# Joining two attention products and reordering the last gates of a fused attention and feed-forward kernel

## The chip, the core and the metric

The kernel runs on one core of a Trainium2 chip. The core has five engines that run their own instruction queues in order: TensorE (PE in the profile; its weight loads are PEld), VectorE (DVE), ScalarE (ACT), GpSimd (POOL) and SyncE (SP), which here issues most DMAs. TensorE writes its products into PSUM, eight banks of 512 fp32 per partition. The metric is the device time of one execution in microseconds (us), as a median of several.

## The reference

All inputs are fp32 (the kernel gets the feed-forward weights as 64-bit floats and converts them itself). Per batch and head, `k` and `v` (576 x 64) give a 64 x 64 matrix `kv`; `q` times `kv` is divided by its root mean square per row; the heads, side by side, are the rows `x` of the feed-forward block:

```python
kv = np.einsum('bhsd,bhse->bhde', k, v)          # 8 batches, 8 heads, 576 tokens, 64 wide
out = np.einsum('bhsd,bhde->bhse', q, kv)
rms = np.sqrt(np.mean(out * out, axis=-1, keepdims=True) + 1e-06)
x = (out / rms * g_norm)                          # -> (4608, 512)
h = ((x @ w1) * (x @ w2)) @ w3                    # 512 -> 1024 -> 1024
y = h @ w_out                                     # 1024 -> 512
```

## The kernel before, in words

**Groups.** The 4608 tokens are worked off in nine groups of 512 (the last 64 tokens of each of the eight batches make up the ninth). The loop takes them in the order T = 0, 1, 2, 3, 4, 5, 6, 8, 7, so the third to sixth groups are T = 2 to 5. `w3 @ w_out` is folded into one matrix at the start. A group then has two stages: the gates, which multiply `x` with `w1` and `w2` and take the elementwise product of the two into a tile `ab`, and the projection of `ab` with the folded matrix, whose result is stored.

**Strassen.** All large products are done with seven block products in place of eight (Winograd's form), with sums of the operand blocks made by VectorE. Blocks are named a11 to a22 and b11 to b22, sums s1 to s4 and t1 to t4, results c11 to c22. From T = 2 on (`IN_TWO`) part of it is done at two levels:
- first gates (`gates(T, 2)`, one level, matmuls at L708),
- gates of two (`gates_of_two`, two levels, L976): 14 products, n = 0 to 6 for w = 0 and again for w = 1, in five banks of the pool `mm`,
- last gates (`gates(T, 3)`, one level, L708): seven products of eight 256-wide matmul records,
- projection (`project_twice`, two levels, L1223): seven inner products of 28 records.

In a one-level stage (`winograd`) a product goes into a bank, `keep` lets ScalarE copy what is needed later to SBUF (L726), further products are accumulated into the same bank after that, and `done` hands two parts to `multiply`: VectorE adds them (L859) and multiplies the two halves into `ab` (L860). Where only one part is given, ScalarE copies one half (L854) and VectorE multiplies it with the other half in PSUM (L856). The order before is: a11 b11 (kept as p1), s1 t1 (kept as p5), s2 t2 (kept as u2), s4 b22 (gives c12), s3 t3 (gives c22 with p5, read from the bank), a12 b21 (gives c11 with p1), a22 t4 (gives c21).

`sum_ab` and `sum_ab_two` (L1069 to L1072) are the operand sums of the projection's outer level, and `sum_inner` (L1181 to L1185) those of its inner level, four operations for each of the seven products n. In the last gates the list `following` says which of them VectorE does after which result.

**Attention between the products.** While group T is worked on, the attention of batch T + 1 is done in eight steps (`steps`). TensorE's order is written out by hand: `between()` runs the next step, twice in the first gates (steps 0 and 1), four times in the gates of two (2 to 5) and twice in the last gates (6 and 7). `begin_kv(g)` multiplies k and v of four heads (L335) into two banks of the pool `at`, ScalarE copies them to `kv_sb` in six copies (L343, L345), and SP is given the loads of the next k and v (L104). `finish(h)` multiplies q with kv for four heads (L413) into two banks, and `norm` squares them on ScalarE (L380, from batch 3 on with one buffer for both halves), reduces (L381), takes the root (L385) and the reciprocal (L387) and scales (L390). For batches 3 to 7, step 1 does `begin_kv(1)` and `finish(0)`, step 4 `finish(1)`, and step 6 `begin_kv(0)` of the batch after; odd batches do `product_left` (L432) in step 3. Here is the choice of banks:

```python
of_mm = b and not (h and b > FIRST_OF_TWO)
o_ps = [bank(*((ps_mm, "mm") if of_mm else (ps_at, "at"))), bank(ps_at, "at")]
```

From batch 2 on, q and x are turned by a ScalarE copy (L296, L294), a DMA transpose (L298) and a second ScalarE copy (L308). `turns_by_scalar` ties them to copies of the gates through `slots`: in the last gates one x copy (L294) follows p1's copy, one follows p5's, and two q copies (L296) of the next batch follow u2's.

**Who sets the order.** TensorE, POOL and SP run in the order of the program (`manual_schedule`). A planner orders ScalarE, and VectorE as well, except in the last gates and the projection from T = 1 on (for T = 8 and 7 from the gates of two on), where VectorE runs in program order. `mm` has five banks and `at` three, given out in turn; a new tile waits for the last use of the bank's old one.

Of the kernel before, what the change touches and what calls it, by code (L numbers as in the profile page):

```python
# [22 lines left out]
def kernel(  # L23
# [294 lines left out]
    def attention(b):  # L318
# [80 lines left out]
        def product(h):  # L399

            of_mm = b and not (h and b > FIRST_OF_TWO)
            o_ps = [bank(*((ps_mm, "mm") if of_mm else (ps_at, "at"))), bank(ps_at, "at")]
            for m in range(4):
                r, e = 2 * h + m // 2, m % 2
                for i in range(2):
                    n = 2 * m + i
                    for t in range(2):
                        tokens = slice(t * L, (t + 1) * L)  # L410
                        for l in range(2):
                            rows = slice(l * D, (l + 1) * D)
                            nc.tensor.matmul(  # L413
                                o_ps[l][tokens, n * D:(n + 1) * D],
                                lhsT=qT[r][rows, e, i, tokens],
                                rhs=kv_b[rows, m // 2 ^ l, e, h, :],
                                start=True,
                                stop=True,
                            )
            xn = st[h] = work.tile([P, 2, 2, 4, D], FP32, name="xn", bufs=1)  # L420
            return norm(o_ps, [xn[:, :, l].rearrange("p i m d -> p m i d") for l in range(2)])
# [151 lines left out]
    def steps(b):  # L573

        a = batch(b)
        a.start()
        more = b + 1 < B  # L580
        fs, ends = ([[] for _ in range(8)] for _ in range(2))

        def turn(i, f, *args, next_group=False):

            t = []

            def begin():
# [12 lines left out]
        by_scalar, in_two = b >= FIRST_OF_TWO, b > FIRST_OF_TWO  # L600
        if b == 1:
            early.extend(a.q_two_by_dma(r) for r in (0, 1))
            q_first = list(early)
            fs[0].append((a.begin_kv, 0))

            def end_first():
                for t in q_first:
                    with tc.issue_after(copies["u3"][-1].ins):
                        next(t)
                    all_of(t)  # L610

            ends[1].append((end_first,))
        fs[2 if b == 1 else 1] += [(a.begin_kv, 1), (a.finish, 0)]
        if b == 1:
            last = {}

            def begin(name, behind, f, *args):
                last[name] = f(*args)
                with tc.issue_after(copies[behind][-1].ins):
                    next(last[name])  # L620
                next(last[name])

            def end(name, behind):
                with tc.issue_after(copies[behind][-1].ins):
                    next(last[name], None)
                all_of(last[name])

            fs[2] += [(begin, f"q{r}", "u2", a.q_two_by_dma, r) for r in (2, 3)]
            fs[3].append((begin, "left", "u3", a.q_left_by_dma))
            fs[4].append((begin, "x", "u3", a.x_by_dma, 0, nc.scalar.copy))  # L630
            ends[4] += [(end, "q2", "p1"), (end, "q3", "p5")]
            ends[5] += [(end, "x", "u2"), (end, "left", "u3")]
        elif by_scalar:
            turns_by_scalar(b)
        else:
            turn(1, a.q_two_by_dma, 2, 3)
            turn(2, a.x_by_dma, 0)
            if odd:
                turn(1, a.q_left_by_dma)
        second = 5 if b == 1 else 4  # L640
        if more:
            fs[6 if in_two else second].append((batch(b + 1).begin_kv, 0))
        fs[second].append((a.finish, 1))
        if odd:
            fs[3 if in_two else second + 1].append((a.product_left,))
        if b == 1:
            turn(6, a.x_by_dma, 1)
# [49 lines left out]

    def winograd(
        lhsT, rhs, chunks, done, between=lambda: None, keep_u3=True, after=lambda: None,
        places=(2, 1, 0),  # L700
    ):


        def product(a_name, b_name, to=None):
            ps = to if to is not None else bank(ps_mm, "mm").rearrange("p (u n) -> p u n", u=2)
            for u in range(2):
                for c in range(chunks):
                    nc.tensor.matmul(  # L708
                        ps[:, u, :],
                        lhsT=lhsT(a_name, u, c),  # L710
                        rhs=rhs(b_name, c),

                        start=(u == 0 and c == 0 and to is None),
                        stop=(c == chunks - 1),
                        skip_group_check=True,
                    )
            after()
            return ps

        def keep(name, ps):  # L720
            if name == "p1":
                t = pair_of_sums[:, 0].rearrange("p s c t -> p (s c) t")
            else:
                t = late_slots(places[("p5", "u2", "u3").index(name)])
            t = t[:, 0:4, :].rearrange("p (u a) n -> p u (a n)", u=2)
            copies.setdefault(name, []).append(nc.scalar.copy(t, ps))  # L726
            run_slot((stage[0], name), copies[name][-1])
            late[name] = t
            return t

        r1 = product("a11", "b11")
        p1 = keep("p1", r1)
        r2 = product("s1", "t1")
        p5 = keep("p5", r2)
        product("s2", "t2", r1)
        u2 = keep("u2", r1)
        between()
        product("s4", "b22", r2)
# [105 lines left out]
    def gates(T, p, between, ready=lambda name: None):  # L844
# [4 lines left out]
        def multiply(name, one, two):  # L849
# [14 lines left out]
            lambda name, c: xb[T][name][:, c, :],  # L864
            NP // 2, done, between, T == 0 or p + 1 < NF,
            places=(2, 1, 0) if T not in IN_TWO else (0, 1, 2) if p + 1 == NF else (2, 0, 1),
        )


# [287 lines left out]

    inner = {}

    def sum_inner(*ns, between=lambda: None):  # L1160

        x_1 = ab[1].rearrange("p f j n -> p j f n")
        if ns == (1, 2):
            x = two_ab_sums[0]
        elif ns == (5, 6):
            x = x_1
        else:
            n, = ns
            x = {0: ab[0][:, :, 0], 3: ab_sums[2], 4: ab[0][:, :, 1], 6: x_1[:, 1]}[n].unsqueeze(1)
        a11, a12, a21, a22 = (  # L1170
            x[:, :, 2 * j:2 * j + 2, i * P:(i + 1) * P] for i in range(2) for j in range(2)
        )
# [2 lines left out]
        else:  # L1175
            s1, s2, s4 = (
                t.unsqueeze(1) for t in (
                    inner_sums[n % 4 // 3] if n < 6 else [pair_of_sums[:, 0, i] for i in range(3)]
                )
            )  # L1180
        nc.vector.tensor_add(s1, a21, a22)  # L1181
        nc.vector.tensor_sub(s2, s1, a11)
        nc.vector.tensor_sub(s4, a12, s2)
        between()
        nc.vector.tensor_sub(a21, a11, a21)  # L1185
        for i, n in enumerate(ns):
            inner[n] = [t[:, i] for t in (a11, a12, a22, s1, s2, s4, a21)]

    def project_twice(T, last, ahead, load_after):
        def store(half):  # L1190
# [245 lines left out]
    for n, T in enumerate(groups):  # L1436
# [44 lines left out]
        for p in range(NF):  # L1481
# [2 lines left out]
            stage[0] = f"p{p}" if T in IN_TWO or T == FIRST_OF_TWO - 1 else None  # L1484
            if T and p + 1 == NF:
                sum_1, sum_2, sum_4, sum_3 = sum_ab(p)
                following = {
                    "c12": [], "c22": [sum_1], "c11": [lambda: sum_inner(0, between=sum_2)],
                    "c21": [*of_two, lambda: sum_inner(1, 2), sum_3, sum_4],
                }  # L1490
# [100 lines left out]
```

## Time and profile before

| | |
|---|---|
| median of 3 runs | 746.61 us (745.99 to 747.71) |
| profiled execution: its time, its span | 747.45 us, 745.7 us |
| granted TensorE clock | 1.0 |
| kernel instructions in the profile | 16769 |
| ScalarE PSUM to SBUF copy of 128x512 (L726) | 61, 587 ns each |
| ScalarE half copy of 128x256 (L854) | 22, 371 ns each |
| VectorE product of 128x256 from PSUM (L856) | 22, 413 ns each |
| VectorE add of 128x512 (L859, mm and inner_sums) | 22, 688 ns each |
| ScalarE q copy before the transpose (L296) | 26, 1058 ns each |
| group T = 3, from its first matmul to the next group's | 313.54 to 386.52 us |

The page gives the share of each engine, the span in 40 slices, the DMA queues, the chain of work that ended last, and the costliest groups of instructions. The chain follows the last instruction back to what released it; the rows "start, length, what" are that chain in order of time. A timeline row has start, length, engine, line, operation, tiles written and read, and in brackets the idle time of the engine before it with what ended it. fp32 matmuls appear as two records each, and a row that merges several shows their number.

### The profile page before, as it was taken

What the parts mean: (1) busy time and instruction counts of PE and PEld (TensorE: products, weight loads), DVE (VectorE), ACT (ScalarE), POOL (GpSimd) and SP (SyncE); (2) the same over time, 40 slices, a digit from 0 to 9 for tenths busy, and PEclk for the clock granted to TensorE, in tenths of its full rate; (3) what the DMA queues carried; (4) which work ended last, traced back from release to release, by engine and by line L of the source; (5) the groups of instructions that cost most, each with busy time, mean ns of one, the idle gap of its engine ahead of it and who ended that gap; (6) DMA issues with size and microseconds to landing.
All of it is one profiled execution on the core that took longest, in us unless ns stands there. A gap on an engine that the chain in (4) does not pass through costs nothing.

```text
span 745.7 us, 16769 instructions
## 1 busy us (share of the span) xinstructions
PE 737.3 (99%) x6843; PEld 658.5 (88%) x6843; DVE 632.7 (85%) x1212; ACT 371.2 (50%) x638; POOL 21.5 (3%) x29
## 2 busy tenths in 40 slices
PE   8999999999999999999999999999999999999998
PEld 5455788888899999999999999999999999999997
DVE  6987998967868699979996999799969987997797
ACT  6687878414552575256526752575267313212321
POOL 0000000131000000010000000000001000000000
PEclk9999999999999999999999999999999999999999
DMA  9996934598999689968987898579847672465454
GB/s 310 365 308 215 263 107 122 124 333 288 275 310 329 172 218 268 312 165 233 276 284 169 252 295 270 179 240 265 290 107 218 209 224 87 157 228 166 133 199 136
DMA packets 135456, 169.65 MB, mean 228 GB/s; under 512 B 78036, under 2 KB 110804, under 8 KB 135380
## 3 DMA queue, kind: packets, MB, share of 16 engines
q1 hardware_dynamic: 132928, 154.16, 68.9%
q10 hardware_dynamic: 2452, 14.42, 5.6%
q8 instruction: 54, 0.88, 0.5%
q14 instruction: 22, 0.18, 0.1%
HBM read 130.55 MB, written 20.71 MB: 203 GB/s over the span
## 4 chain that ended last, share of the span: by engine, by line
PE 94%; DMA 2%; DVE 1%; ACT 1%; issue 0%; SPq 0%; ACTq 0%; DVEq 0%
PE mm L708 38%; PE mm L1223 22%; PE mm L976 21%; PE mm L682 7%; PE at L335 2%; PE at L413 1%; DMA raw<-in_moe_w_out_dram 1%; PE at L669 1%; DMA w3o_sb<-w3o_l 1%; PE mm L413 1%; DMA raw<-in_moe_w_dram 0%; PE at L1266 0%; PE at L432 0%; ACT w_sb L133 0%; DVE c L859 0%; ACT qT L296 0%
## 5 line engine op out<-in xcount | busy, mean ns | idle before, releaser
L1025 ACT COPY slots<-mm 128x512 f32<-128x512 f32 x88 | 51.6, 586 | 131.4 <-PE mm L1223 73.4
L708 PE MATMUL mm<-xT,w_sb 128*128 128x256 f32 x480 | 110.2, 379 | 0.0
L708 PEld LDWEIGHTS mm<-xT,w_sb 128*128 128x128 f32 x480 | 90.4, 190 | 12.1 <-issue 0.5
L708 PE MATMUL mm<-xc,ws 128*128 128x256 f32 x352 | 79.8, 380 | 0.9 <-ACT inner_sums L726 0.9
L708 PEld LDWEIGHTS mm<-xc,ws 128*128 128x128 f32 x352 | 66.9, 190 | 10.2 <-ACT inner_sums L726 1.3
L726 ACT COPY slots<-mm 128x512 f32<-128x512 f32 x61 | 35.8, 587 | 70.9 <-PE mm L708 66.7
L682 PE MATMUL mm<-chunks,ab 128*128 128x512 f32 x128 | 60.7, 605 | 1.2 <-DVE chunks L172 1.2
L1029 DVE TENSOR_TENSOR slots<-mm,slots 128x512 f32<-128x512 f32 x66 | 45.3, 686 | 17.7 <-PE mm L976 17.3
L1026 ACT COPY slots<-mm 128x384 f32<-128x384 f32 x88 | 42.4, 482 | 24.9 <-PE mm L1223 22.3
L976 PE MATMUL mm<-ws,w3o_sb 128*128 128x128 f32 x350 | 54.0, 275 | 0.0
L1223 PE MATMUL mm<-w3o_sb,ab 128*128 128x128 f32 x368 | 48.7, 275 | 0.2 <-DMA w3o_sb<-w3o_l 0.2
L976 PEld LDWEIGHTS mm<-ws,w3o_sb 128*128 128x128 f32 x350 | 46.4, 192 | 0.0
L1223 PEld LDWEIGHTS mm<-w3o_sb,ab 128*128 128x128 f32 x368 | 45.4, 192 | 0.8 <-issue 0.4
L381 DVE TENSOR_REDUCE inv<-sq 128x8 f32<-128x512 f32 (+1 forms) x40 | 24.5, 628 | 25.3 <-ACT sq L380 25.0
L1223 PE MATMUL mm<-w3o_sb,raw 128*128 128x128 f32 x340 | 43.5, 275 | 0.0
L708 PE MATMUL mm<-xc,w_sb 128*128 128x256 f32 x176 | 42.4, 384 | 0.3 <-ACT slots L726 0.3
L682 PEld LDWEIGHTS mm<-chunks,ab 128*128 128x128 f32 x128 | 21.6, 190 | 22.9 <-issue 14.3
L1223 PEld LDWEIGHTS mm<-w3o_sb,raw 128*128 128x128 f32 x340 | 40.7, 192 | 0.0
L708 PE MATMUL mm<-xT,ws 128*128 128x256 f32 x160 | 38.5, 384 | 0.0
L708 PEld LDWEIGHTS mm<-xc,w_sb 128*128 128x128 f32 x176 | 32.8, 190 | 5.3 <-ACT slots L726 0.7
L1030 DVE TENSOR_TENSOR slots<-mm,slots 128x384 f32<-128x384 f32 x66 | 36.4, 551 | 0.9 <-PE mm L1223 0.9
L854 ACT COPY c<-mm 128x256 f32<-128x256 f32 x22 | 8.2, 371 | 54.1 <-PE mm L708 51.2
(230 smaller groups left out, 1634.2 us busy)
## 6 DMA issues: line engine op xcount, KB each, us to landing
w3o_sb<-w_l SPq DMA_DIRECT2D x21, 896.0 KB, 5.3
w3o_sb<-w3o_l SPq DMA_DIRECT2D x18, 896.0 KB, 4.7
raw<-in_moe_w_dram SPq DMA_DIRECT2D x31, 512.0 KB, 7.8
raw<-w3o_l SPq DMA_DIRECT2D x15, 896.0 KB, 4.8
w3o_sb<-w3o_l ACTq DMA_DIRECT2D x14, 896.0 KB, 4.7
k_sb<-in_k_dram SPq DMA_DIRECT2D x16, 576.0 KB, 4.9
v_sb<-in_v_dram SPq DMA_DIRECT2D x16, 576.0 KB, 6.1
q_sb<-in_q_dram SPq DMA_DIRECT2D x32, 256.0 KB, 4.5
```

Source lines behind the costliest of these rows:

```text
L335: nc.tensor.matmul(ps[r * D:(r + 1) * D, :], lhsT=k_sb[rows, r, cols], rhs=v_sb[rows, r, cols], start=(j == 0), stop=(j == JS - 1),)
L381: adds["norm"] = nc.vector.tensor_reduce(out=inv[:, i], in_=sq.rearrange("p (h d) -> p h d", d=D), axis=AX.X, op=ALU.add)
L413: nc.tensor.matmul(o_ps[l][tokens, n * D:(n + 1) * D], lhsT=qT[r][rows, e, i, tokens], rhs=kv_b[rows, m // 2 ^ l, e, h, :], start=True, st ...
L682: nc.tensor.matmul(sums_ps[half][m], lhsT=w3T[half, c][:, m, :], rhs=chunks[:, c, 1, :], start=(c == 0), stop=(c == KF - 1),)
L708: nc.tensor.matmul(ps[:, u, :], lhsT=lhsT(a_name, u, c), rhs=rhs(b_name, c),  start=(u == 0 and c == 0 and to is None), stop=(c == chunks ...
L726: copies.setdefault(name, []).append(nc.scalar.copy(t, ps))
L976: nc.tensor.matmul(ps[place // 4][:, place % 4, :], lhsT=x, rhs=y, start=new and place // 4 not in seen, stop=True, skip_group_check=True,)
L1025: nc.scalar.copy(z[:, 0:4], ps[0])
L1026: return nc.scalar.copy(z[:, 4:7], ps[1][:, 0:3])
L1029: nc.vector.tensor_add(z[:, 0:4], ps[0], z[:, 0:4])
L1030: nc.vector.tensor_add(z[:, 4:7], ps[1][:, 0:3], z[:, 4:7])
L1223: nc.tensor.matmul(ps[place // 4][:, place % 4, :], lhsT=x[:, c, :], rhs=y[:, c, :], start=new and place // 4 not in seen, stop=(c == 1), ...
```

## The change

Three parts:

1. For batches 3 to 6 (groups T = 2 to 5), `begin_kv(0)` of the next batch moves from step 6 to step 4, ahead of `finish(1)`. The loads of the k and v after it, which `begin_kv` issues, move along. `finish(1)` now takes its first bank from `mm`.
2. In the last gates of all groups from T = 2 on, a11 b11 is no longer kept in SBUF. ScalarE copies it from its bank into a second bank, and a12 b21 is accumulated there, so that the bank holds c11 and needs no add: ScalarE copies one half, VectorE multiplies. The order of the products becomes a11 b11, s1 t1, s2 t2, a12 b21 (c11), s3 t3 (c22), s4 b22 (c12), a22 t4 (c21). For T = 2 to 5 the first bank comes from `at`.
3. `sum_inner` is split into single steps. The sums of products 1 and 2 are made one product at a time (four operations of 256 each in place of four of 512 for both), and all of them are spread over the last gates in another order.

```diff
-            of_mm = b and not (h and b > FIRST_OF_TWO)
+            of_mm = b and (h == 0 or b < B - 1)
...
-            fs[6 if in_two else second].append((batch(b + 1).begin_kv, 0))
+            fs[second].append((batch(b + 1).begin_kv, 0))
...
+        if copy_first:
+            r1 = halves(first if first is not None else bank(ps_mm, "mm"))
+            r3 = halves(bank(ps_mm, "mm"))
+            product("a11", "b11", r1, new=True)
+            copies["p1"].append(nc.scalar.copy(r3, r1))
+            run_slot((stage[0], "p1"), copies["p1"][-1])
+            r2 = product("s1", "t1")
+            p5 = keep("p5", r2)
+            product("s2", "t2", r1)
+            u2 = keep("u2", r1)
+            between()
+            product("a12", "b21", r3)
+            done("c11", r3, None)
+            product("s3", "t3", r1)
+            done("c22", p5, r1)
+            product("s4", "b22", r2)
+            between()
+            done("c12", r2, u2)
+            product("a22", "t4", r1)
+            done("c21", r1, None)
+            return
...
+            copy_first=T in IN_TWO and p + 1 == NF,
+            first=bank(ps_at, "at") if T in IN_TWO and p + 1 == NF and T + 2 < B else None,
...
-    def sum_inner(*ns, between=lambda: None):
+    def steps_of_inner(*ns):
...
+        return [
+            lambda: nc.vector.tensor_add(s1, a21, a22),
+            lambda: nc.vector.tensor_sub(s2, s1, a11),
+            lambda: nc.vector.tensor_sub(s4, a12, s2),
+            lambda: nc.vector.tensor_sub(a21, a11, a21),
+        ]
+
+    def sum_inner(*ns, between=lambda: None):
+        *others, replace = steps_of_inner(*ns)
+        all_of(f() for f in others)
+        between()
+        replace()
...
+            zero, one, two = (steps_of_inner(n) for n in range(3)) if T in IN_TWO else [None] * 3
             following = {
+                    "c11": zero[0:3], "c22": [],
+                    "c12": [sum_1, sum_3, sum_2, one[0], zero[3], one[1]],
+                    "c21": [
+                        one[2], one[3], *of_two, two[0], sum_4, two[1], two[2], two[3],
+                    ],
+                } if T in IN_TWO else {
                     "c12": [], "c22": [sum_1], "c11": [lambda: sum_inner(0, between=sum_2)],
                     "c21": [*of_two, lambda: sum_inner(1, 2), sum_3, sum_4],
                 }
```

More of the change, by code (lines that the diff above doesn't have):

```diff
@@ L699, in winograd, with halves, product @@
         lhsT, rhs, chunks, done, between=lambda: None, keep_u3=True, after=lambda: None,
-        places=(2, 1, 0),
+        places=(2, 1, 0), copy_first=False, first=None,
     ):
-        def product(a_name, b_name, to=None):
-            ps = to if to is not None else bank(ps_mm, "mm").rearrange("p (u n) -> p u n", u=2)
+        def halves(ps):
+            return ps.rearrange("p (u n) -> p u n", u=2)
+        def product(a_name, b_name, to=None, new=False):
+            new = new or to is None
+            ps = halves(bank(ps_mm, "mm")) if to is None else to
             for u in range(2):
@@ L711, in product @@
                         rhs=rhs(b_name, c),
-                        start=(u == 0 and c == 0 and to is None),
+                        start=(u == 0 and c == 0 and new),
                         stop=(c == chunks - 1),
@@ L1168, in sum_inner @@
             n, = ns
-            x = {0: ab[0][:, :, 0], 3: ab_sums[2], 4: ab[0][:, :, 1], 6: x_1[:, 1]}[n].unsqueeze(1)
+            x = {
+                0: ab[0][:, :, 0], 1: ab_sums[0], 2: ab_sums[1], 3: ab_sums[2], 4: ab[0][:, :, 1],
+                6: x_1[:, 1],
+            }[n].unsqueeze(1)
         a11, a12, a21, a22 = (
@@ L1177, in sum_inner @@
                 t.unsqueeze(1) for t in (
-                    inner_sums[n % 4 // 3] if n < 6 else [pair_of_sums[:, 0, i] for i in range(3)]
-                )
-            )
[L1181 to L1185, printed above, removed]
+                    [pair_of_sums[:, n % 2, i] for i in range(3)] if n in (1, 2, 6)
+                    else inner_sums[n % 4 // 3]
+                )
+            )
         for i, n in enumerate(ns):
             inner[n] = [t[:, i] for t in (a11, a12, a22, s1, s2, s4, a21)]
+        return [
[9 more added lines that the diff above has]
+        replace()
     def project_twice(T, last, ahead, load_after):
```

## The prediction, made before the result was known

> **What bounds the kernel now.** I read the page's busy times and its chain first, then the chain in order of time, then the timelines of three engines around the last gates of one group, T=3.
>
> ```profile
> PE 737.3 (99%) x6843; PEld 658.5 (88%) x6843; DVE 632.7 (85%) x1212; ACT 371.2 (50%) x638; POOL 21.5 (3%) x29
> ...
> PE 94%; DMA 2%; DVE 1%; ACT 1%; issue 0%; SPq 0%; ACTq 0%; DVEq 0%
> ```
>
> TensorE is busy for 99% of the span and is 94% of the chain, at full granted clock in every slice. An edit elsewhere counts only where it makes TensorE wait. The chain shows whether it waits:
>
> ```profile
> 323.90 1.21 PE at L335 x72
> ...
> 326.05 1.93 PE mm L708 x8
> 327.97 15.63 PE mm L976 x140
> 343.60 1.09 PE at L413 x64
> 344.69 6.45 PE mm L976 x56
> 351.14 5.18 PE mm L708 x24
> 356.32 1.21 PE at L335 x72
> 357.53 7.10 PE mm L708 x32
> 364.63 21.89 PE mm L1223 x196
> ...
> 583.80 22.22 PE mm L1223 x196
> 606.03 12.09 PE mm L708 x56
> 618.12 21.88 PE mm L976 x196
> ```
>
> The columns are start, length, work. The last two rows give undisturbed rates: 12.09/56 = 0.216 us per L708 matmul and 21.88/196 = 0.1116 per L976 matmul. Group T=3 (first eight rows) runs at these rates but for the small 64x64 products between them; its projection takes 21.89. Only T=6 (583.80) shows 0.34 us more. So before, TensorE hardly waits in the changed stretch. The margins lie with the other two engines, here ScalarE and then VectorE:
>
> ```profile
> 326.49 0.60 ACT L380 ACTIVATE sq<-mm 128x512 f32<-128x512 f32 x1
> ...
> 355.21 0.58 ACT L726 COPY slots<-mm 128x512 f32<-128x512 f32 x1 [0.77 <-DVE ab L1062]
> ...
> 357.12 2.00 ACT L296 COPY qT<-q_sb 128x1024 uint16<-128x1024 uint16 x2
> 359.01 0.22 ACT L343 COPY kv_sb<-at 128x64 f32<-128x64 f32 x1
> ```
>
> ```profile
> 346.94 0.69 DVE L381 TENSOR_REDUCE inv<-sq 128x8 f32<-128x512 f32 x1 [0.88 <-ACT sq L380]
> ...
> 358.32 0.94 DVE L1071 TENSOR_TENSOR ab<-ab 128x768 f32<-128x768 f32 x1
> 359.56 0.69 DVE L859 TENSOR_TENSOR c<-mm,slots 128x512 f32<-128x512 f32 x1 [0.30 <-PE mm L708]
> ...
> 361.22 0.69 DVE L859 TENSOR_TENSOR c<-slots,mm 128x512 f32<-128x512 f32 x1 [0.51 <-PE mm L708]
> ```
>
> VectorE runs from the second reduce (346.94) to the end of L1071 without idle time, is then just early for c12 and c22 (0.30 and 0.51 idle), and c22's add ends at 361.91, while a22 t4, which overwrites the bank it reads, starts at 362.75: 0.84 us spare.
>
> **Part 1, the join.** The joined form stands in the trace at step 1: from 323.90 to 327.97, less 8 matmuls (1.73), 2.34 us. Apart they cost: product 343.60 to 351.14 less 56 x 0.1116 = 1.29; k v 351.14 to 364.63 less 56 x 0.216 = 1.40. Together 2.69. The join saves 0.35 us in each of T=2 to 5, all on TensorE's path: 1.4 us.
>
> **Part 2, what the moved work puts in front of the last gates (T=3).** On TensorE step 4 starts at 343.53 and takes 2.15 us (323.83 to 325.98 in step 1), 1.06 more than now. So the last gates start at 352.04 (350.98 before), each product 1.73 later: a12 b21 at 357.23, s3 t3 358.96, s4 b22 360.69, a22 t4 362.41.
>
> ScalarE: the six k v copies now stand before the squares. In step 1 the first square came 2.66 us after the k v product's start (323.83 to 326.49), so it starts at 346.19 instead of 344.74. The second square uses the same buffer and waits for the first reduce (step 1: 0.81 idle on it). Square 346.19 to 346.79, reduce 346.82 to 347.51 (0.69), second square 347.60 to 348.20, second reduce from 348.24: 1.30 late. VectorE has no idle time behind it; one gap of 0.03 closes: L1071 starts at 359.59, and VectorE is free at 360.46 (0.87 later, as L1070 to L1071).
>
> ScalarE again: p5's copy waits for L1062 and comes at 356.48, L294 0.48 later, u2's copy at 357.91, the two L296 from 358.39, and what follows them 1.89 later (357.12 to 359.01). That is now c11's half copy: 360.28, ending 360.65 (0.37, row L854). In the old order nothing urgent was behind the pair.
>
> VectorE: c11's product starts at 360.68; three inner sums, each reading the one before, 0.46 apart (rows L860 to L1181 to L1182): 361.14, 361.60, 362.06; then c22's add 0.34 later (as L1183 to L767, 365.05 to 365.39) at 362.40, ending 363.09. TensorE wants that bank at 362.41. It starts 0.06 after (T=6: L1185 ends 589.62, matmul 589.68) and loses 0.10 in restarting (that product took 0.55 for four matmuls, not 0.45). Loss: 363.15 + 0.10 - 362.41 = **0.84 us**. With the join, +0.49 per group; the VectorE rows of T=2, 4 and 5 lie within 0.05 of T=3's relative to step 4, so x 4 = +2.0.
>
> The Trainium skill (PSUM — Partial Sum Buffer, Engine vs sequencer instructions) says that ScalarE's and VectorE's queues are strict FIFO, which speaks against this change: c11's copy cannot pass the q copies. The rows agree (359.01 is right behind the pair). Were it otherwise, VectorE's 360.46 alone would decide and the loss would be 0.62, the sum +1.1 instead of +2.0.
>
> **Part 3, the other groups.** T=6 has no q copies and no join. VectorE is free at 579.81 (L1071 578.94 + 0.87), c22's add would run from 581.53 to 582.21, and a22 t4 is wanted at 571.55 + 6 x 1.728 = 581.92: 0.45 lost with restart. Its present loss of 0.34 (TensorE waits for the pair's third and fourth sums, ends 589.02 and 589.62) goes, because the sums of 1 alone are ready near 587. Net +0.1. In T=8 and 7 the add ends at 650.12 against 650.21 wanted (and 718.06 against 718.15): nothing.
>
> **What I cost at nothing, with its cover.**
> - The copy from bank to bank isn't in the trace. The nearest row is the same copy into SBUF, 0.587 us; the shortest ScalarE copy here is 0.2 us and the longest about 1.2. It starts near 353.97, and p5's copy can't start before 356.48; with L294 (1.05) there is 1.4 us for it. I take 0.59; without this cover the excess would go to u2's copy.
> - c11 loses a 0.69 add, and the pair of 512 (2.65 us) becomes eight of 256 (about 3.1). They end about 5.5 us after the projection starts, before 6.2; the third product wants them at 7.6.
> - SP: k and v loads (576 KB each, 5 to 6 us to landing) now go ahead of three w3o loads (347.82 to 351.34) and, in T=2 and 4, a transpose of x_left. The w3o loads are needed from 364 on: 7 us of cover even if all wait for k and v. POOL's copies of x_left come later still.
> - Step 4's product takes a bank that VectorE's add frees at 342.98, and starts at 344.63. Its k and v were issued at 325.2 and 325.6, 18 us ahead.
>
> The Trainium skill (ScalarE: Activation LUTs, Step-by-step: what each stage is for) holds that ScalarE writes faster to PSUM than to SBUF; no run here shows it yet, and with this cover it would change nothing.
>
> **Sum.** -1.4 + 3.4 + 0.1 = +2.1 us. The profiled execution took 747.45 (span 745.7), 0.84 above the median of 746.61; added to the median: **748.7 us**.
>
> **Rivals.**
> - *The join's gain stays (faster).* If c22's add ends by 362.35, only -1.4 and T=6's -0.34 remain: 744.9. Place: the start of c11's product, which must be 0.74 earlier, at 359.94 or before; both ScalarE's 360.65 and VectorE's 360.46 would have to be too late by my count. For it: the planner's old order left 0.84 spare at this spot. Against: no idle time in 12 us of VectorE.
> - *About even.* The loss is only 0.2 to 0.6, because the squares come up to 0.3 earlier or the q copies overlap the wait: between -0.5 and +1.1: about 746.9.
> - *A second wait.* u2's copy ends at 358.50, and s3 t3, which overwrites that bank, is wanted at 358.96: 0.46 spare. A bank-to-bank copy near 2 us, or a lag 0.5 larger, makes this wait too and moves all behind it: about +0.5 per group, 750.7. Near it in price: the join saves nothing between 128-wide matmuls as in step 4 (+3.5, 750.1).
>
> **How the numbers follow.** Forecast 0.55 (own range +1.2 to +3.2: 747.8 to 749.8, from 0.2 us per group on the loss); faster rival 0.12; even 0.15; second wait or no saving 0.18. The range leaves out the faster rival and the far end of the last: 745.7 to 750.8. A measurement here can tell 0.2%, 1.5 us, from no change: faster 0.12; the even case and the low end of the forecast, same 0.26; slower 0.62.
>
> **What would show it.** Right: in T=2 to 5 the last product of the last gates (the L712 matmuls that read xc and w_sb into an `at` bank) waits for VectorE's add by 0.7 to 0.9 us; ScalarE's L854 comes straight behind the two L296; step 4 as one piece of 2.3 us; projections of 21.9 in all groups, T=6 included. Wrong: ScalarE reaching c11's copy before 359.7, VectorE's second reduce less than 1 us late, or a wait at s3 t3 or in the projection that I don't have.

## The result, and the profile after

The changed kernel takes 750.48 us (median of 6 runs, 750.15 to 750.66) against 746.76 us before (6 runs, 745.99 to 747.71): a ratio of 1.005, 95% interval 1.0037 to 1.0063. It is slower by 0.5%, or 3.7 us, where I had forecast 2.1. The profiled execution took 750.66 us with a span of 748.9, 3.2 us longer than before's.

In the changed kernel the lines have moved: the one-level products are L712 (L708 before), the gates of two L1004 (L976), the projection L1262 (L1223), the half copy L880 (L854), its product L882 (L856), the add L885 (L859), the copies of `keep` L730 (L726), the inner sums L1216 to L1219 (L1181 to L1185), the last of the sums of two L1099 (L1071). The copy from bank to bank is L739.

The page of the changed kernel, busy times and the chain by engine:

```profile
PE 737.2 (98%) x6843; PEld 657.5 (88%) x6843; DVE 629.4 (84%) x1233; ACT 373.9 (50%) x645; POOL 21.5 (3%) x29
...
PE 81%; DVE 9%; ACT 6%; issue 2%; DMA 1%; SPq 0%; POOL 0%; ACTq 0%; DVEq 0%
```

TensorE's work is the same, 737.2 us against 737.3, but its share of the chain fell from 94% to 81%: the chain now leaves TensorE and goes through VectorE and ScalarE. Where it does so is seen in the chain in order of time for T=3 (columns: start, length, work):

```profile
344.18 1.28 PE at L335 x72
...
346.77 0.60 ACT sq L380
...
347.40 0.70 DVE inv L381
...
358.44 0.59 ACT slots L730
359.03 0.70 ACT qT L296
...
359.87 1.05 ACT qT L296
360.92 0.28 ACT c L880
...
361.23 0.43 DVE ab L882
...
361.68 0.43 DVE raw L1216
...
362.14 0.43 DVE raw L1217
...
362.60 0.43 DVE raw L1218
363.02 0.61 DVE c L885
...
363.68 1.99 PE at L712 x8
365.67 21.89 PE mm L1262 x196
```

From the first product of the joined piece (step 4, with the k v product straight ahead of the q kv product; 344.18) the chain runs over the k v copies, the first square and its reduce, on through the queues of ScalarE and VectorE to u2's copy (358.44), and over the two q copies, c11's half copy, c11's product, the three inner sums and c22's add, and only then comes back to TensorE for a22 t4 (363.68). Three timelines of the same group give the margins:

```profile
360.12 0.95 DVE L1099 TENSOR_TENSOR ab<-ab 128x768 f32<-128x768 f32 x1
361.23 0.42 DVE L882 TENSOR_TENSOR ab<-c,mm 128x256 f32<-128x256 f32 x1 [0.16 <-ACT c L880]
...
361.24 1.89 PE L712 MATMUL mm<-xT,ws 128*128 128x256 f32 x8
363.68 1.99 PE L712 MATMUL at<-xc,w_sb 128*128 128x256 f32 x8 [0.54 <-DVE c L885]
```

s4 b22 starts at 361.24 and a product lasts 1.73, so a22 t4 was wanted at 362.97. It came at 363.68, 0.71 late, and took 1.99 in place of 1.89: a loss of 0.81 us. c11's product was held by ScalarE for the last 0.16 us, by VectorE's own queue until then.

The table has each group's period, the time from its first L712 matmul to the next group's, read from TensorE's timeline of each profile. Starts cancel out in it, and it repeats to 0.01 us where nothing is changed, so it shows far smaller effects than the total time.

| us | T=2 | T=3 | T=4 | T=5 | T=6 | T=8 |
|---|---|---|---|---|---|---|
| before | 73.80 | 72.98 | 73.79 | 72.98 | 72.73 | 67.95 |
| after | 74.26 | 73.43 | 75.31 | 73.43 | 72.84 | 68.00 |
| three sums behind c22 | 73.45 | 72.62 | 74.37 | 72.62 | 72.39 | 67.95 |
| no join | 74.40 | 73.53 | 74.41 | 73.54 | 72.84 | 68.01 |
| join alone | 73.91 | 73.09 | 74.59 | 73.09 | 72.73 | 67.95 |
| join, split sums | 73.55 | 72.74 | 74.34 | 72.74 | 72.40 | 67.94 |
| q copies behind c11 | 74.01 | 73.20 | 74.43 | 73.19 | 72.83 | 68.00 |
| q product first | 76.32 | 75.24 | 76.34 | 75.24 | 72.83 | 68.01 |
| 15 fewer warm-ups | 73.44 | 72.63 | 73.45 | 72.62 | 72.39 | 67.95 |
| 4 fewer warm-ups | 73.44 | 72.62 | 73.57 | 73.37 | 72.39 | 67.94 |

After minus before: 0.46, 0.45, **1.52**, 0.45, 0.11, 0.05, and 0.07 for T=7, taken to the span's end. T=4 stands out by 1.06 us, of which 0.1 is a longer wait at a22 t4 (0.64 in place of 0.54). What makes the rest appears in TensorE's load timeline, in the middle of T=4's joined piece:

```profile
421.19 0.13 PEld L413 LDWEIGHTS at<-kv_sb,qT 64*64 64x64 f32 x1 [0.78 <-issue]
```

"Issue" means that the engine waited for nothing that the profile shows. I call this idle stretch the hole. 131 of the piece's 136 matmul records stand ahead of the hole. I had not foreseen it.

### The profile page after: what moved, and what is told of

The parts are those of the page before. It is cut to its first block, busy times and chain, and to the rows that moved or that the text cites. A ratio compares the mean times of both kernels' runs of the same rounds, so it can differ in the third digit from the quotient of the medians.

```text
span 748.9 us, 16800 instructions
## 1 busy us (share of the span) xinstructions
PE 737.2 (98%) x6843; PEld 657.5 (88%) x6843; DVE 629.4 (84%) x1233; ACT 373.9 (50%) x645; POOL 21.5 (3%) x29
## 4 chain that ended last, share of the span: by engine, by line
PE 81%; DVE 9%; ACT 6%; issue 2%; DMA 1%; SPq 0%; POOL 0%; ACTq 0%; DVEq 0%
PE mm L712 29%; PE mm L1262 22%; PE mm L1004 17%; PE mm L682 7%; PE at L335 2%; ACT xT L308 1%; ACT qT L296 1%; PE at L712 1%; DVE xn L390 1%; PE at L669 1%; ACT slots L730 1%; PE mm L413 1%; DMA raw<-in_moe_w_out_dram 1%; PE at L413 1%; DVE c L885 1%
## 5 line engine op out<-in xcount | busy, mean ns | idle before, releaser
L1053 ACT COPY slots<-mm 128x512 f32<-128x512 f32 x88 | 51.5, 586 | 128.9 <-PE mm L1262 74.7
L712 PE MATMUL mm<-xT,w_sb 128*128 128x256 f32 x416 | 95.7, 379 | 0.0
L712 PEld LDWEIGHTS mm<-xT,w_sb 128*128 128x128 f32 x416 | 78.4, 190 | 10.8 <-issue 0.5
L712 PE MATMUL mm<-xc,ws 128*128 128x256 f32 x320 | 72.9, 379 | 0.1
L730 ACT COPY slots<-mm 128x512 f32<-128x512 f32 x57 | 33.4, 586 | 71.7 <-PE mm L712 66.8
L712 PEld LDWEIGHTS mm<-xc,ws 128*128 128x128 f32 x320 | 60.7, 190 | 8.7 <-ACT inner_sums L730 0.5
L1004 PE MATMUL mm<-ws,w3o_sb 128*128 128x128 f32 x350 | 53.9, 275 | 0.0
L1262 PE MATMUL mm<-w3o_sb,ab 128*128 128x128 f32 x368 | 48.7, 275 | 0.8 <-DVE raw L1086 0.8
L1262 PEld LDWEIGHTS mm<-w3o_sb,ab 128*128 128x128 f32 x368 | 45.4, 192 | 1.3 <-DVE raw L1086 0.9
L1004 PEld LDWEIGHTS mm<-ws,w3o_sb 128*128 128x128 f32 x350 | 46.4, 192 | 0.0
L1262 PE MATMUL mm<-w3o_sb,raw 128*128 128x128 f32 x340 | 43.5, 275 | 0.0
L1262 PEld LDWEIGHTS mm<-w3o_sb,raw 128*128 128x128 f32 x340 | 40.7, 192 | 0.0
L712 PE MATMUL mm<-xT,ws 128*128 128x256 f32 x160 | 38.1, 381 | 0.0
L712 PE MATMUL mm<-xc,w_sb 128*128 128x256 f32 x144 | 35.1, 386 | 0.5 <-ACT slots L730 0.3
L308 ACT COPY xT<-xn 128x1024 uint16<-128x1024 uint16 x28 | 32.5, 1168 | 3.4 <-DMA xn<-xT 3.4
L712 PEld LDWEIGHTS mm<-xT,ws 128*128 128x128 f32 x160 | 30.2, 190 | 4.2
```

Source lines behind the costliest of these rows:

```text
L308: copy(words(dst), src)
L712: nc.tensor.matmul(ps[:, u, :], lhsT=lhsT(a_name, u, c), rhs=rhs(b_name, c),  start=(u == 0 and c == 0 and new), stop=(c == chunks - 1), s ...
L1004: nc.tensor.matmul(ps[place // 4][:, place % 4, :], lhsT=x, rhs=y, start=new and place // 4 not in seen, stop=True, skip_group_check=True,)
L1053: nc.scalar.copy(z[:, 0:4], ps[0])
L1262: nc.tensor.matmul(ps[place // 4][:, place % 4, :], lhsT=x[:, c, :], rhs=y[:, c, :], start=new and place // 4 not in seen, stop=(c == 1), ...
```

## The experiments

The kernel before was run again with them; its median was 746.98 us beside experiments 1 to 3 and 6, and 747.07 beside 4, 5 and the bigger shifts of 7. The ratios below are to these.

**1. The three sums behind c22.** Is it the three inner sums, put ahead of c22's add, that TensorE waits for?

```diff
-                    "c11": zero[0:3], "c22": [],
+                    "c11": [], "c22": zero[0:3],
```

> The changed kernel, with the three inner sums of product 0 moved from behind c11 to behind c22 on VectorE; ScalarE's and TensorE's order are as in the changed kernel. Theory (the three sums stand between c11's product and c22's add, and TensorE waits for that add): c11's product ends 17.54 us after the last gates' stage of T=3 began to be late (344.11 in the changed kernel's profile), the add follows at once and ends 18.3, before a22 t4 is wanted at 18.86. The wait of 0.71 and the restart of 0.10 go in T=2 to 5 (3.2 us) and 0.45 in T=6: about 750.5 - 3.7 = 746.8 us, 746.2 to 747.3. Rival (a22 t4 is held by VectorE's general lag, so that a shorter queue in front of the add only moves the wait to c12's or c21's sums and the projection): less than 1 us is gained, 749.5 or more, and the projections of T=2 to 5 grow by 0.4 to 0.8 us each. The 0.78 us hole in the joined piece of T=4: if it belongs to the place in TensorE's instruction stream, it stays, since that stream is unchanged.

Measured: 746.12 us (11 runs; against before 0.9992, 95% 0.9983 to 1.0001), 0.1 below my range. Its chain through T=3's last gates does not leave TensorE:

```profile
358.26 1.73 PE at L712 x8
359.99 1.73 PE mm L712 x8
361.71 1.73 PE at L712 x8
363.44 21.88 PE mm L1262 x196
```

The periods fall by 0.81 in T=2, 3 and 5 and by 0.45 in T=6, the very losses that the prediction had worked out (0.84 and 0.45, both with the restart), and the projection stays at 21.88. Moving three operations whose result is needed only in the projection took 4.4 us off the median. The groups' periods account for 3.9 of that; 0.6 us of the difference between the two profiles lies ahead of T=2, where the edit changes nothing. T=4 stays 0.92 above T=2: the hole is another matter.

**2. The join undone.** The new last gates and sums stay.

```diff
-            fs[second].append((batch(b + 1).begin_kv, 0))
+            fs[6 if in_two else second].append((batch(b + 1).begin_kv, 0))
...
-            of_mm = b and (h == 0 or b < B - 1)
+            of_mm = b and not (h and b > FIRST_OF_TWO)
...
-            first=bank(ps_at, "at") if T in IN_TWO and p + 1 == NF and T + 2 < B else None,
+            first=None,
```

> The changed kernel without the join: the next batch's k v product stands in step 6 again and the first bank of finish(1) and of the last gates is taken as before; the new last gates and the split inner sums stay. Theory: the two small products cost 0.35 us more in each of T=2 to 5 (+1.4); the last gates start 1.06 us earlier and VectorE's lag of 0.87 us is gone; but the six k v copies (1.3 us, 359.01 to 360.32 in the profile of before) now stand on ScalarE between the two q copies and c11's half copy, so that copy ends near 360.7, c22's add near 363.1, and a22 t4, wanted near 362.75, still waits about 0.35 and 0.1 for the restart. Against before: +0.45 x 4 + 0.1 (T=6) = +1.9, 748.7 us (747.8 to 749.6). Rival (the wait comes from the join alone, by its late squares): no wait is left, and the time is before's plus 0.1, 746.9 us. T=4's hole of 0.78 us should be gone in either case, if it belongs to the joined piece.

Measured: 750.02 us (5 runs; against before 1.0043, 1.0030 to 1.0055), 0.4 above my range. T=4's hole is gone (74.41 beside T=2's 74.40). The chain of T=3 shows the order that I had expected:

```profile
357.41 1.89 ACT qT L296 x2
359.30 0.11 ACT kv_sb L343
...
360.54 0.38 ACT c L880
...
360.94 0.43 DVE ab L882
...
362.74 0.61 DVE c L885
...
363.39 1.99 PE mm L712 x8
```

The six k v copies stand between the q copies and c11's half copy. The periods are 0.55 to 0.62 above before's, where I had expected 0.45; that is 0.5 us over four groups, and 0.1 more in T=8 and 7. The rest is open: a wait of 1.1 us for a w3o load ahead of T=2 is in this profile, but T=2 starts no later than in before's (239.18 and 239.58 us). So the new last gates lose 0.55 to 0.62 a group by themselves, where with the join they lose 0.81, and by other copies in the same place: the rival that blamed the join alone is out.

**3. The join alone**, with the old last gates and sums (the first bank of the last gates from `at`).

```diff
-            fs[6 if in_two else second].append((batch(b + 1).begin_kv, 0))
+            fs[second].append((batch(b + 1).begin_kv, 0))
...
-        r1 = product("a11", "b11")
+        r1 = product(
+            "a11", "b11", None if first is None else first.rearrange("p (u n) -> p u n", u=2), new=True,
+        )
```

> The join alone: the kernel before, with the next k v product in step 4, the banks that go with it (the last gates' first bank from at), and the old last gates and inner sums. Theory: 0.35 us is saved in each of T=2 to 5. VectorE is 0.87 us late at the last gates as in the changed kernel, but c12's and c22's adds stand directly one behind the other; c22's ends 18.8 us after the reference point at which a22 t4 is wanted at 18.9, so there is no wait, or one of less than 0.1. Before - 1.4 = 745.4 us (745.0 to 746.3, the upper end with T=4's hole of 0.8 us). Rival (VectorE's lag costs TensorE a wait in the old order too, or the join saves nothing between 128-wide matmuls): 746.8 or more.

Measured: 748.77 us (10 runs; 1.002, 1.0011 to 1.003). The rival was right: the periods are 0.11 above before's, not 0.35 below. 0.46 is lost again. Two timelines of T=3 show where:

```profile
363.08 1.99 PE L709 MATMUL at<-xc,w_sb 128*128 128x256 f32 x8
...
368.03 1.50 PE L1227 MATMUL mm<-raw 128*128 128x128 f32 x12
369.37 1.70 PE L1227 MATMUL mm<-raw,inner_sums 128*128 128x128 f32 x12
370.96 0.71 PE L1227 MATMUL mm<-raw 128*128 128x128 f32 x4
...
368.88 0.69 DVE L1186 TENSOR_TENSOR inner_sums<-inner_sums,raw 128x512 f32<-128x512 f32 x1
369.61 0.69 DVE L1187 TENSOR_TENSOR inner_sums<-raw,inner_sums 128x512 f32<-128x512 f32 x1
```

c22's add costs 0.11 at a22 t4 (1.99, not 1.89), just over what I had allowed; 0.35 is lost in the projection's second inner product, which reads the pair's sums while VectorE is still making them (1.70 and 0.71 in place of 1.50 and 0.61). VectorE is later here because the k v copies put the second reduce back. I had looked at the last gates and not at the sums behind them, though the prediction had priced the same wait in T=6 at 0.34.

**4. The join alone with the sums of 1 and 2 made apart**, the changed kernel's third part without its second.

```diff
-                    "c21": [*of_two, lambda: sum_inner(1, 2), sum_3, sum_4],
+                    "c21": [*of_two, *one, *two, sum_3, sum_4],
```

> The join with the old last gates, as in the run of the join alone, and the inner sums of products 1 and 2 made one after the other, s of 1 first (eight operations of 256 in place of four of 512), followed by the third and fourth outer sums as before. Theory (in the join alone, VectorE's lag of 0.87 us costs 0.11 at a22 t4 and 0.35 in the projection, whose second inner product waits for the pair's sums): product 1's sums are ready 0.8 us earlier, the 0.35 in the projection of T=2 to 6 goes, the 0.11 stays; the outer sums end 1.05 later, still ahead of the third product. Periods of T=2, 3, 5: 0.24 less than before's (0.11 more in the join alone); T=6 0.34 less than before's; time: that of the join alone minus 4 x 0.35 + 0.34, 747.0 us (746.2 to 747.8). Rival (the projection then waits for the outer sums, or the 0.35 has another cause): 748.3 or more.

Measured: 746.93 us (11 runs; 0.9999, 0.9991 to 1.0008), periods 0.24 to 0.25 below before's in T=2, 3 and 5, 0.33 below in T=6, as expected. From the chain:

```profile
362.40 1.84 PE at L709 x8
364.24 21.88 PE mm L1238 x196
```

The projection is back at 21.88. The 0.11 at a22 t4 is still lost (1.84 in place of 1.73). So the join does pay 0.35 a group once the sums of product 1 no longer wait for those of product 2, and 0.24 of it is left after that loss.

**5. The q copies behind c11's half copy.** Can ScalarE's order alone take the wait away?

```diff
-                at(("p3", "u2"), begin, ("q", b + 1, r), n.q_by_dma, r)
+                at(("p3", "c11" if b > FIRST_OF_TWO else "u2"), begin, ("q", b + 1, r), n.q_by_dma, r)
```

> The changed kernel with the two q copies of the next batch (1.89 us on ScalarE) tied to c11's half copy instead of u2's copy in T=2 to 5, so that they stand behind the half copy. TensorE's and VectorE's order is as in the changed kernel. Theory (both engines are late at c11's product, ScalarE by the q copies and VectorE by its own queue only 0.16 us less): the half copy comes when a12 b21 ends, 1.2 us earlier than in the changed kernel, but VectorE ends L1099 at 361.07 in T=3 of the changed kernel's profile, so c11's product starts 0.13 to 0.16 earlier and no more; the wait of a22 t4 falls from 0.71 to about 0.56. Changed kernel - 4 x 0.15 = 749.9 us (749.4 to 750.4). Rival (the q copies alone make the wait): the wait goes, changed kernel - 4 x 0.81 = 747.2 us.

Measured: 749.49 us (5 runs; 1.0032, 1.0020 to 1.0045). T=3's timelines of ScalarE, VectorE and TensorE:

```profile
358.30 0.59 ACT L730 COPY slots<-at 128x512 f32<-128x512 f32 x1
359.62 0.37 ACT L880 COPY c<-mm 128x256 f32<-128x256 f32 x1 [0.74 <-PE mm L712]
359.89 1.99 ACT L296 COPY qT<-q_sb 128x1024 uint16<-128x1024 uint16 x2
...
360.85 0.42 DVE L882 TENSOR_TENSOR ab<-c,mm 128x256 f32<-128x256 f32 x1
...
363.29 1.99 PE L712 MATMUL at<-xc,w_sb 128*128 128x256 f32 x8 [0.31 <-DVE c L885]
```

The half copy now waits for TensorE (0.74) and ends 0.86 before VectorE comes to it. The wait shrinks by 0.23 to 0.25 a group, not by 0.81: two engines were late at the same point, and freeing one leaves the other.

**6. The q kv product ahead of the k v product** in the joined piece, so that the squares come first on ScalarE. In this order the kernel no longer computes the reference's result, for a cause that was not found, so its run says something of waits alone.

```diff
-        if more:
-            fs[second].append((batch(b + 1).begin_kv, 0))
+        if more and not in_two:
+            fs[second].append((batch(b + 1).begin_kv, 0))
         fs[second].append((a.finish, 1))
+        if more and in_two:
+            fs[second].append((batch(b + 1).begin_kv, 0))
```

> The changed kernel with the two products of the joined piece in the other order for batches 3 to 6: first the second q kv product, then the next batch's k v. The k v copies then stand behind the squares on ScalarE, and the squares start 1.05 us earlier. Theory (the lag of VectorE and of p5's, u2's and the q copies comes from the k v copies in front of the squares): VectorE is free 0.8 us earlier; ScalarE's u2 copy comes when its product ends, 0.58 earlier, and c11's half copy with it; c22's add ends 0.5 to 0.6 earlier, the wait of a22 t4 shrinks from 0.71 to 0.1 to 0.2 us. Changed kernel - 4 x 0.55 = 748.3 us (747.6 to 749.2). Rival (c11's copy is held by something else on ScalarE): 750.0 or more. T=4's hole of 0.78 us: if it comes from 136 small matmuls in a row, one of that size is to be seen again, at whatever place; if it is a matter of the k v loads or of chance, not.

Measured: 757.56 us, and periods 1.8 to 2.1 above the changed kernel's in T=2, 3 and 5. The waits of T=3 show what took the place of the lag (who waited for whom: us in total, times, longest):

```profile
PEld at L714 <- DVE c L887: 1.3, 1, 1.3
...
PE at L714 <- DVE c L887: 0.9, 1, 0.9
...
PEld mm L1006 <- ACT slots L1055: 0.7, 1, 0.7
...
PE mm L1006 <- ACT slots L1055: 0.5, 1, 0.5
```

The planner put both squares, the root and the six k v copies ahead of the next copy of the gates of two, so TensorE waits for that copy in the middle of the gates of two, which it had never done, and everything behind comes later. The experiment changed ScalarE's order more than I meant; it does not decide its question.

**7. The hole, by its place in TensorE's program.** Experiments 1 and 3 to 6 have such a hole too, all in T=4, with 131 to 133 of the 136 records ahead of it. The page names a queue that moves program text:

```profile
q8 instruction: 54, 0.88, 0.5%
```

The columns are packets, MB and share. 0.88 MB over TensorE's 2 x 6843 records is 64 bytes a record, and 54 packets are 16.3 KB each: some 256 records, loads and matmuls together. The Trainium skill (Perfetto Trace Analysis, The 4-stage abstract model) gives 64 bytes to an instruction, which agrees. The joined piece has 272. The idea: a packet edge lies at the 6th instruction of T=4's piece, the next at the 262nd, and the packet that begins there isn't in yet, as 256 small instructions last 1.9 us. It is tested by shifting the whole program: two warm-up matmuls fewer or more at the very start.

```diff
-        keep_warm(14)
+        keep_warm(12)
```

> The kernel with the three sums behind c22, with two warm-up matmuls fewer at the very start (12 in place of 14): 8 TensorE instructions fewer ahead of everything, nothing else. In that kernel 131 of the 136 matmul records of T=4's joined piece stand ahead of its hole. Theory (the hole stands at an edge in TensorE's program): the edge moves back in the piece by 8 instructions, 4 matmul records: 135 records stand ahead of the hole in T=4, or it falls on the piece's very end. Rival (the hole belongs to a time or to DMA traffic): 131, as before, give or take one.

> The same with two warm-up matmuls more (16 in place of 14), 8 TensorE instructions more ahead of everything. Theory of the edge: 127 of the 136 records stand ahead of T=4's hole; the edge before it then lies 2 instructions ahead of the piece, so that the hole may be a little shorter. Rival: 131.

T=4's hole with two fewer, and then with two more:

```profile
418.27 0.13 PEld L413 LDWEIGHTS at<-kv_sb,qT 64*64 64x64 f32 x1 [0.97 <-issue]
```

```profile
419.15 0.13 PEld L413 LDWEIGHTS at<-kv_sb,qT 64*64 64x64 f32 x1 [0.68 <-issue]
```

With two fewer, 135 records stand ahead of the hole; with two more, 127; with neither, 131. Both as expected, to the record (one run each: 745.39 and 746.43 us). So the hole belongs to a place in the program, not to a time or to another transfer. That this place is an edge between packets is inferred from their size and from their times in the traces: the changed kernel's 54 packets start 252 TensorE records apart on average, 255 with the wait records of its queue counted. In each of the nine profiles with a hole, one packet starts 0.06 to 0.61 us after the piece's first load, and TensorE goes on 2.24 to 2.48 us after that start, 1.4 to 1.6 us after the packet's end. The later the packet starts, the longer the hole, in the main: 0.42 us for a start 0.11 us into the piece (experiment 5), 0.78 for 0.35 (the changed kernel), 0.97 for 0.61 (two fewer). An edge near a piece's start is not enough: counted on by 256 from T=4's hole, one falls within two instructions of the start of step 1's piece in T=2 and T=6 of the changed kernel too. Neither piece has a hole, and their packets start 3.0 and 2.8 us ahead of them. Two bigger shifts, on top of experiment 1:

```diff
-    def keep_warm(n):
+    def keep_warm(n, wide=0):
...
+        for _ in range(wide):
+            four = ident.unsqueeze(1).to_broadcast([P, 4, P])
+            nc.tensor.matmul(
+                t.rearrange("p (k n) -> p k n", k=4), lhsT=ident, rhs=four, start=True, stop=True
+            )
...
-        keep_warm(14)
+        keep_warm(9, 1)
```

> The kernel with the three sums behind c22, and 4 fewer warm-up matmuls at the very start (one of 512 columns in place of four, and one taken out), so that 16 fewer TensorE instructions stand ahead. Theory of the packet's edge: T=4's edge moves from the 6th to the 22nd instruction of the joined piece, the next would be the 278th of 272: T=4's hole goes. T=5's edge moves from the 246th (10 before the piece began) to the 6th: T=5 gets the hole, at the 262nd to 264th instruction, four or five matmul records before the piece's end, as T=4 had it. T=4's period falls by 0.9 us and T=5's grows by 0.9; the time is that of the kernel with the three sums behind c22 within 0.4 us. Rival (the hole belongs to T=4 or to its DMA traffic): it stays in T=4 and T=5 has none.

Measured: T=4's period falls to 73.57, T=5's grows by 0.75 to 73.37, and the hole is in T=5's piece:

```profile
491.63 0.13 PEld L418 LDWEIGHTS at<-kv_sb,qT 64*64 64x64 f32 x1 [0.57 <-issue]
```

It moved to the group that I had named, but 122 records stand ahead of it, not 131, and T=4 keeps 0.13. I had counted only loads and matmuls between the two pieces; 18 further instructions there would explain the difference. The Trainium skill (Perfetto Trace Analysis, Identifying Dependency Chains) says that instructions waiting on several engines may have further ones inserted ahead of them. The traces of experiment 1 and of this run have 17 wait records (EVENT_SEMAPHORE) on TensorE's queue from one piece to the other, which moves the expected place from the 262nd to the 245th instruction, 122 records. The time was 747.05 us (11 runs; 0.9999, 0.9990 to 1.0008), 0.9 more than in experiment 1, where I had allowed 0.4; its profile has a wait of 1.5 us for a w3o load ahead of T=2, experiment 1's one of 0.5, but the two profiled executions differ by 0.2 us only, so the cause stays open.

```diff
-        keep_warm(14)
+        keep_warm(2, 3)
...
-        keep_warm(9)
+        keep_warm(1, 2)
```

> The kernel with the three sums behind c22, and 15 fewer warm-up matmuls at the very start: five groups of four 128-wide ones are replaced by five of 512 columns, so that TensorE's time at the start is about the same but 60 fewer instructions stand ahead of everything (a program matmul is four records, two loads and two matmuls). Theory (the page's queue of kind instruction, 54 packets of 16.3 KB for 13.7 thousand TensorE records, is TensorE's own program, 64 bytes each, 256 to a packet; the hole in T=4's joined piece stands at its 262nd to 264th instruction of 272 because a packet's edge lies at its 6th, the next one at its 262nd, and the 256 between are small and are used up in 1.9 us, before the next packet is in): with 60 fewer in front, the edge lies at T=4's 66th and no other piece of 68 small matmuls has one before its 16th; no hole of over 0.4 us is left in any joined piece. T=4's period falls by 0.92 us, to T=2's. 746.1 - 0.9 = 745.2 us (744.6 to 745.8). Rival (the hole is one of DMA traffic or of what stands in T=4): it stays in T=4, and the time too.

Measured: **745.31 us** (11 runs; against before 0.9983, 95% 0.9974 to 0.9992), the lowest median of all versions, 0.2% below the kernel before and 0.7% below the changed one. T=4 takes 73.45, as T=2 does, and its joined piece is followed by the gates of two without a hole; TensorE's load timeline there:

```profile
415.51 1.14 PEld L340 LDWEIGHTS at<-v_sb,k_sb 64*64 64x64 f32 x72
417.65 0.52 PEld L1009 LDWEIGHTS mm<-xc,w3o_sb 128*128 128x128 f32 x4
```

The gates of two go on 2.14 us after the piece's first load. In the changed kernel T=4's piece took 3.1 us (418.36 to 421.46 in TensorE's timeline).

## Why the prediction was right, and what it missed

The forecast of 748.7 us was 1.8 too low, and its mechanism is the one that the profile shows. The whole range, 745.7 to 750.8, held with 0.3 us to spare; the forecast's own part of it, 747.8 to 749.8, did not. The 750.48 lies in the part that stood for the rivals of a second wait and of no saving, neither of which came. That the total fell inside is in part luck: the hole in T=4, which I did not foresee, and differences outside the groups brought it there. Times of T=3 below are compared after taking off the 0.58 us by which the group starts later in the changed kernel's profile (313.96 against 313.38).

- **Part 1, the join.** 0.35 saved in each group: the periods of experiment 1, which has no wait left in these groups, lie 0.35 to 0.36 under before's in T=2, 3 and 5. Right. The Trainium skill (TensorEngine Tiling (Array Packing), Key Properties) says that a change of tiling mode drains TensorE; one piece of 64x64 matmuls less between 128-wide ones agrees with it in sign, and 0.35 us is what it measured here; no run separates the drain from other costs of the switch.
- **Part 2, the lag.** The second reduce came 1.23 late (predicted 1.30), L1099 1.22 (1.27). c11's half copy: 360.23 (360.28). c11's product: 360.65 (360.68), last held by ScalarE, as said. c22's add ends 363.04 (363.09). a22 t4 starts at 363.10 (363.15), wanted at 362.39 (362.41). Loss 0.81 (0.84), net 0.45 to 0.46 a group (0.49). Right, term by term, and experiment 1 takes just that away.
- **ScalarE keeps its order.** The half copy is right behind the q copies (360.81, in the chain 360.92), and experiment 5 shows the other half of the argument: without the q copies in front, VectorE alone still costs 0.57 a group, where the prediction had 0.62 for that case.
- **Part 3.** T=6 +0.11 (+0.1), and both of its terms: with experiment 1 its period is 0.34 under before's. T=8 and 7 were put at nothing, with 0.09 us spare; each lost 0.05 there: the add ends in time (0.11 us ahead in T=8), but a22 t4 takes 1.94 in place of 1.89, so a margin of 0.1 us is not quite free.
- **What was costed at nothing.** The bank-to-bank copy measured 0.570 us (0.59 assumed) and made nothing wait. The same copy into SBUF is 0.586 in this profile; the Trainium skill (ScalarE: Activation LUTs, Step-by-step: what each stage is for) has the sign right, and the gain is 3%. The split sums, the k and v loads and step 4's bank cost nothing, as said; T=6 even shows that the split is worth 0.34.
- **The term that was missing.** The sum had no price for the joined piece beyond its 2.34 us, taken from step 1's pieces in the profile of before. Those show no hole. T=4's has one; that group lost 1.06 us beyond the others, nearly a third of the profile's 3.2. With it the sum would have been 3.2 and the forecast 749.8. The rest of the measured 3.7 is 0.1 in T=8 and 7, 0.1 at the start, and some 0.5 by which the two profiled executions stand differently to their medians.
- **The rivals.** None came. The join's gain did not stay, u2's bank held up nothing (s3 t3 runs straight on at 359.51), and the join does save. The time of the second-wait rival, 750.7, is near the measured one by accident only: its place shows no wait.

Open: what sets a packet's start, 0.06 us into the joined piece in one run, 0.61 in another and 3 us ahead of step 1's pieces, and what fills the 1.4 to 1.6 us between a packet's end and TensorE's next instruction.

## What to carry to other kernels

Before an add that frees a bank for the next product, put nothing whose result is needed only later; work out for each such point when *both* engines that lead to it come free, since moving one alone may gain only part of the loss (0.24 of 0.81 us in experiment 5). When VectorE gets later, follow it past the stage in question, to the sums of the next one. And a run of small matmuls that is longer than one packet of the program (some 256 instructions, by the sizes here) may stall TensorE, when its packet starts late, at a place that shifts with every instruction added ahead of it: look for "issue" idle time in the middle of such runs, in each group, before a difference is put down to the edit.

## What the hardware showed that I had not expected

- TensorE stops for 0.4 to 1.0 us inside a run of 272 small instructions, at a place of its own program that moves by exactly four matmul records for two matmuls taken out far ahead (135, 131, 127 records). The Trainium skill (Trainium Architecture — The Big Picture, The software stack) has the instruction streams brought to the engines when the program is loaded. Here 54 packets of kind instruction, 16.3 KB each, arrive while it runs, so not all of TensorE's is there at the start; one such hole (0.92 us) is 0.1% of the time.
- The hole's length does not follow from its place: after 131 records it was 0.78 us in the changed kernel, 0.75 in experiment 1 and 0.42 in experiment 5, one profile each. Its end does follow the packet, 2.24 to 2.48 us after the packet's start in all nine profiles.
- A product that waits for a bank pays the wait and then 0.10 us more over its eight matmul records (1.99 against 1.89 us); an add that ended 0.11 us before its bank was wanted still cost 0.05 (1.94, T=8).
